# Four logit steps a unit instead of five, logits in five PSUM banks and half a borrowed one

## The chip, the cores and the metric

The kernel runs on one core of a Trainium2 chip. The core has a matrix engine (TensorE, PE in the profile; PEld are its weight loads), three engines for element-wise work (VectorE, DVE; ScalarE, ACT; GpSimd, POOL) and a queue that issues DMAs (SyncE, SP). They run at the same time and wait for each other by semaphores. Matmuls write to PSUM, eight banks of 512 fp32 columns on 128 partitions; DVE and ACT read PSUM, POOL and DMAs don't. The metric is the device time of one execution, in microseconds.

## What is computed

```python
xn = layernorm(x)                          # x: 2048 x 512, four segments of 512 rows
# A: attention with a memory; 32 heads of 16; for each segment
logits = q k^T / 4 + causal mask;  p = softmax(logits);  a_dot = p v
a_mem  = phi(q) M / (phi(q) z + 1e-6)      # phi(t) = t + 1 if t > 0 else exp(t)
o      = sigmoid(beta) a_mem + (1 - sigmoid(beta)) a_dot
M += phi(k)^T v;  z += sum of phi(k)       # carried to the next segment
s      = o wo
# B: g = silu(relu(xn w1) w2), w1: 512 x 1792
out = x + s * g
```

All in fp32. q, k, v are xn times wq, wk, wv (512 x 512).

## The kernel before

Matrix products in full precision are made of three fp32r matmuls of a number's high and low part (`triple`, lines 610 to 612): high x high, low x high, high x low. Weights come by DMA into `raw`, ACT copies the high part (L397), POOL subtracts for the low one (L398). The MLP (`mlp`), the projections of q and k (`proj`), values (`vproj`), output (`wout`) and memory (`memory`, `numden`) all run in this way on three PSUM banks `pd`.

The softmax works on *units* of four heads: 8 units a segment, 32 in all. A unit's rows stand in `qs` and `ks`, two heads in the two 64-row halves of the partitions and two planes p, put there by DMAs (`stack`, L909). Each row has a fourth part for its negative maximum, so that the exponential needs no other operand. So logits are made twice: first with queries as rows for the maxima (`rowmax`, into `pS`, two banks), then, with the maxima in place, transposed (`expo`, into `pT`, two banks), for ACT to take exponentials into `P` (L1026, L1020). Only blocks on and below the diagonal are made: widths 128, 256, 384 and 512. The two heads of a plane are a pair of matmuls that run side by side.

In `rowmax`, DVE reduces the part off the diagonal out of pS (L956), ACT copies the diagonal blocks to `rd` (L955), POOL masks these (L958), DVE reduces them (L961). At a unit's end DVE joins the maxima and splits them (L967 to L970), `maxrows` transposes them on PE (L977), ACT copies (L979), and two DMAs put them into qs. In `expo`, POOL clears what lies above the diagonal in P (L1016). `pv` multiplies P with the values into the bank `pO` (L1060); ACT scales (L1075), and DMAs and `combine` divide and merge with the memory's part.

A loop over steps t writes the order of PE: five steps a unit (tables RSTEP, ESTEP), in each the maxima's logits of unit u and the exponentials' logits of a unit LAG = 9 steps behind, and the values' product of a unit in two bursts (steps 0 and 2). Between these visits stands filler work, MLP and projections, dealt out by a budget. For the other engines a planner (class `Sched`) keeps a list of pending operations, each with a duration and a due time (the last number of `act`, `dve`, `pool`, `dma`), and writes the earliest due of those that could start. The semaphores are set later, from the order in which instructions touch tiles.

Of the kernel before, what the change touches and what calls it, by code (L numbers as in the profile page):

```python
# [7 lines left out]
F32 = mybir.dt.float32  # L8
# [17 lines left out]
LAG = 9  # L26
RESERVE = 13.00
M3 = 0.70
ND0 = 3
SOON = 0.21  # L30
SWITCH = 0.40


RSTEP = (((0, 3, 0),), ((0, 0, 0), (0, 2, 128)), ((0, 1, 0), (1, 1, 256)), ((1, 0, 0), (1, 2, 128)), ((1, 3, 0),))
ESTEP = (((0, 0, 0),), ((1, 0, 0),), ((0, 1, 0), (0, 3, 384)), ((1, 1, 0), (1, 3, 384)), ((0, 2, 0), (1, 2, 256)))
# [20 lines left out]
class Sched:  # L56
# [108 lines left out]
    def avail(self, rd, wr):  # L165
        t = 0.0
        ops = [self.W.get(k) for k in (*rd, *wr)]
        for k in wr:
            ops += self.R.get(k, ())
        for o in ops:  # L170
            if o is not None and o.eng != "PE":
                t = max(t, o.t if o.out else self.now + 3.31)
        return t
# [31 lines left out]
def emit(PE, ACT, DVE, POOL, SP, cst, ps, dr, args, plan, left):  # L205
# [38 lines left out]
    class Banks(Ring):  # L244

        def two(self):
            done = [(t, k) for t, k in self.t if k not in S.W or S.R.get(k)]
            return sorted(done, key=lambda b: S.avail((), (b[1],)))[:2]

        def next(self):  # L250
            return self.two()[0]

# [7 lines left out]
    S.free["POOL"] = 1.4  # L260
    identr = cst.tile([128, 128], F32R, name="identr")
    magic = cst.tile([128, 4], I32, name="magic")
    blk = cst.tile([128, 128], F32, name="blk")
    gcol = cst.tile([128, 4], F32, name="gcol")
# [10 lines left out]
    MM = [cst.tile([128, 128], F32R, name=f"mm{i}") for i in range(2)]  # L275
    Mbd = [cst.tile([128, 128], F32, name=f"mbd{g}") for g in range(4)]
    zbd = [cst.tile([128, 128], F32, name=f"zbd{g}") for g in range(4)]
# [5 lines left out]
    PDR = Banks("pd", [128, 512], F32, 3, ps)  # L283
    PSR = Ring("pS", [128, 2, 512], F32, 1, ps)
    PTR = Ring("pT", [128, 2, 512], F32, 1, ps)
    POR = Ring("pO", [128, 512], F32, 1, ps)
# [9 lines left out]
    EXR = Ring("ex", [128, L], F32)  # L296
# [4 lines left out]
    EER = Ring("ee", [128, L], F32)  # L301
# [9 lines left out]
    PR = [Ring(f"P{i}_", [128, 4, 512], F32) for i in range(2)]  # L311
# [6 lines left out]
    MV = Ring("mv", [128, 4, 2], F32, 2)  # L318
    RS = Ring("rs", [128, 4], F32, 2)
    NW = Ring("nw", [128, 2, 4], F32, 2)  # L320
# [5 lines left out]
    def consts():  # L326
        for i in range(NS):
            ks = stack_rows(i)
            pool(950, (), ks, lambda i=i: POOL.memset(r32(QS[i]), 0.0), 9.3 + 8 * i, 1e-3)
            pool(950, (), ks, lambda i=i: POOL.memset(r32(KS[i]), 1.0), 16.2 + 8 * i, 1e-3)  # L330
        pool(0, (), ["zrow"], lambda: POOL.memset(zrow, 0.0), 34.6)
        for i in range(2):
            pool(500, (), [f"mm{i}"], lambda i=i: POOL.memset(r32(MM[i]), 0.0), 51.4 + 5 * i, 1e-3)
        dve(128, (), ["identr"], lambda: DVE.tensor_copy(identr, ident), 53.4)
        for i in range(2):
            pool(500, (), [f"v{i}{t}" for t in range(4)],
                 lambda i=i: POOL.memset(VT[i][:, :, :, 16:32], 1.0), 33.1 + 20 * i, 1e-3)
        pool(100, (), ["blk"], lambda: POOL.memset(blk, 1.0), 46.8, 1e-3)
        b3 = blk.rearrange("p (b r) -> p b r", r=16)
        pool(128, ["blk"], ["blk"], lambda: POOL.affine_select(  # L340
            b3, b3, pattern=[[-16, 8], [0, 16]], compare_op=OP.is_ge, fill=0.0, base=0, channel_multiplier=1), 51.1)
        pool(128, ["blk"], ["blk"], lambda: POOL.affine_select(
            b3, b3, pattern=[[16, 8], [0, 16]], compare_op=OP.is_ge, fill=0.0, base=15, channel_multiplier=-1), 52.1)
        pool(10, (), ["magic"], lambda: POOL.memset(magic, 0x5f3759df), 66.0)

    def gates():
        for h in range(8):
            dma((), [f"gcol{h}"], lambda h=h: SP.dma_start(gcol[16 * h:16 * h + 16], bass.AP(
                tensor=beta.tensor, offset=beta.offset + h, ap=[[0, 16], [8, 4]])), 45.4)
        for b in range(4):  # L350
            dma((), [f"gsc{b}"], lambda b=b: SP.dma_start(gsc[32 * b:32 * b + 32], bass.AP(
                tensor=beta.tensor, offset=beta.offset + b, ap=[[0, 32], [4, 8]])), 47.5)
        pool(10, (), ["pari"], lambda: POOL.iota(pari, pattern=[[0, 2]], base=0, channel_multiplier=1), 53.8)
# [1022 lines left out]
```

## Time and profile before

| | us |
|---|---|
| median of 3 runs (lowest, highest) | 800.14 (797.95, 801.23) |
| profiled execution | 799.96 |
| its span, first to last instruction | 798.2 |
| PE busy | 767.3 |
| DVE, ACT, POOL busy | 474.7, 488.9, 484.8 |

Granted TensorE clock: 0.99 in the mean. A group row of the profile gives line, engine, operation, output<-inputs, shapes and count; then busy time and the mean length of one in ns; then idle time ahead of them with what ended it. A row of waits reads: who waited <- for whom: us in all, times, longest. fp32 matmuls stand in the trace as two records each.

### The profile page before, as it was taken

Reading aid. Unit: us, or ns where it says so; the run is one execution under the profiler, and the core shown is the slowest. Engines: PE = TensorE matmul, PEld = TensorE weight load, DVE = VectorE, ACT = ScalarE, POOL = GpSimd, SP = SyncE. Lnnn points to the kernel's source line nnn. Section 1 sums busy time; section 2 is a strip of 40 time slices with the busy share of each in tenths; the row PEclk is TensorE's granted clock in tenths of the full one; section 3 lists DMA queues with packets and bytes.
Section 4 is the critical chain, followed back from the end, with each engine's and each line's share of the span. In section 5 each row is a group of like instructions: output and inputs, shape, how many; then the busy total and the mean of one; then the engine's idle time right before and its main releaser. Section 6 shows DMA issues by size and latency. Waiting matters only on the chain.

```text
span 798.2 us, 14187 instructions
## 1 busy us (share of the span) xinstructions
PE 767.3 (96%) x4726; PEld 535.3 (67%) x4726; DVE 474.7 (59%) x838; ACT 488.9 (61%) x828; POOL 484.8 (61%) x585
## 2 busy tenths in 40 slices
PE   7999999999999999998999999999899989999996
PEld 6787677777676856575676766676576756665664
DVE  4336886546466765555655885664566445656546
ACT  4454757557766666567577576667367665665561
POOL 6735656556566555857467384866466566776474
PEclk9999999999999999999999999999899999999999
DMA  4345434355445445543454536544335447643233
GB/s 140 108 130 145 144 101 132 85 140 157 105 123 162 126 134 152 176 116 113 125 155 143 145 98 198 154 115 141 103 95 157 129 134 207 177 121 107 78 93 119
DMA packets 110632, 105.45 MB, mean 132 GB/s; under 512 B 23568, under 2 KB 73744, under 8 KB 110560
## 3 DMA queue, kind: packets, MB, share of 16 engines
q1 hardware_dynamic: 110480, 104.46, 45.2%
q8 instruction: 37, 0.61, 0.3%
q14 instruction: 35, 0.29, 0.1%
q10 hardware_dynamic: 80, 0.10, 0.0%
HBM read 65.44 MB, written 8.72 MB: 93 GB/s over the span
## 4 chain that ended last, share of the span: by engine, by line
PE 80%; DVE 5%; DMA 5%; POOL 4%; issue 4%; ACT 1%; SPq 1%; POOLq 0%; DVEq 0%; ACTq 0%
PE pd L610 19%; PE pd L611 15%; PE pd L612 15%; PE pO L1060 9%; PE pS L936 8%; PE pT L1009 4%; PE pd L595 4%; POOL wl L398 2%; PE pd L884 2%; DMA gsc<-in_A_beta_dram 1%; POOL rd L958 1%; DVE mn L956 1%; DVE hl L635 1%; PE pd L562 1%; PE pd L862 1%
## 5 line engine op out<-in xcount | busy, mean ns | idle before, releaser
L398 POOL TENSOR_TENSOR wl<-raw,wh 128x512 fp32r<-128x512 f32 x176 | 226.3, 1293 | 77.4 <-ACT wh L397 74.9
L956 DVE TENSOR_REDUCE mn<-pS 128x2 f32<-128x768 f32 (+2 forms) x160 | 127.0, 794 | 129.6 <-ACT rd L955 83.9
L958 POOL TENSOR_SCALAR_AFFINE_SELECT rd<-rd 128x512 f32<-128x512 f32 (+1 forms) x160 | 88.4, 553 | 153.1 <-ACT rd L955 151.0
L610 PE MATMUL pd<-xh,wh 128*128 128x512 f32 x352 | 147.6, 419 | 2.9 <-ACT vt L601 1.1
L955 ACT ACTIVATE rd<-pS 128x512 f32<-128x512 f32 (+1 forms) x160 | 82.0, 512 | 98.3 <-PE pS L936 85.6
L1026 ACT ACTIVATE P<-pT 128x1024 f32<-128x1024 f32 x128 | 131.1, 1024 | 15.0 <-PE pT L1009 14.0
L611 PE MATMUL pd<-xl,wh 128*128 128x512 f32 x352 | 137.7, 391 | 0.2 <-DVE xl L570 0.2
L612 PE MATMUL pd<-xh,wl 128*128 128x512 f32 x352 | 137.9, 392 | 0.0
L961 DVE TENSOR_REDUCE md<-rd 128x4 f32<-128x512 f32 (+1 forms) x160 | 92.0, 577 | 57.4 <-POOL rd L958 55.9
L397 ACT ACTIVATE wh<-raw 128x512 fp32r<-128x512 f32 x174 | 106.5, 630 | 10.1 <-DMA raw<-in_A_wk_dram 2.7
L1016 POOL TENSOR_SCALAR_AFFINE_SELECT P<-P 128x512 f32<-128x512 f32 x128 | 82.8, 656 | 35.1 <-ACT P L1026 31.0
L610 PE MATMUL pd<-wh,hh 128*128 128x512 f32 x224 | 95.4, 426 | 3.6 <-DVE kl L788 2.6
L936 PEld LDWEIGHTS pS<-ks,qs 64*128 64x128 f32 x512 | 40.7, 185 | 74.3 <-issue 40.2
L611 PE MATMUL pd<-wl,hh 128*128 128x512 f32 x224 | 88.0, 393 | 0.0
L612 PE MATMUL pd<-wh,hl 128*128 128x512 f32 x224 | 87.9, 393 | 0.0
L610 PEld LDWEIGHTS pd<-xh,wh 128*128 128x128 f32 x352 | 66.1, 188 | 30.8 <-issue 9.9
L936 PE MATMUL pS<-ks,qs 64*128 64x256 f32 (+3 forms) x512 | 83.9, 385 | 2.0 <-DVE mn L956 1.0
L1060 PE MATMUL pO<-P,vt 128*32 128x512 f32 (+3 forms) x1024 | 83.5, 442 | 0.8 <-POOL P L1016 0.8
L612 PEld LDWEIGHTS pd<-xh,wl 128*128 128x128 f32 x352 | 66.1, 188 | 14.8
L611 PEld LDWEIGHTS pd<-xl,wh 128*128 128x128 f32 x352 | 66.3, 188 | 11.3 <-DVE xl L570 0.5
L1009 PE MATMUL pT<-qs,ks 64*128 64x384 f32 (+3 forms) x512 | 64.7, 310 | 0.0
L610 PEld LDWEIGHTS pd<-wh,hh 128*128 128x128 f32 x224 | 42.1, 188 | 26.9 <-issue 7.6
(143 smaller groups left out, 1173.6 us busy)
## 6 DMA issues: line engine op xcount, KB each, us to landing
raw<-in_B_w_dram SPq DMA_DIRECT2D x112, 256.0 KB
qs<-qh SPq DMA_DIRECT2D x128, 64.0 KB
ks<-kh SPq DMA_DIRECT2D x128, 64.0 KB
io<-in_A_x_dram SPq DMA_DIRECT2D x28, 256.0 KB
raw<-in_A_wq_dram SPq DMA_DIRECT2D x16, 256.0 KB
raw<-in_A_wk_dram SPq DMA_DIRECT2D x16, 256.0 KB
raw<-in_A_wv_dram SPq DMA_DIRECT2D x16, 256.0 KB
qs<-ql SPq DMA_DIRECT2D x64, 64.0 KB
```

The costliest lines, as they stand in the source:

```text
L397: act(512, [rk], [hk], lambda: ACT.activation(h, raw, AF.Copy), 6.3)
L398: pool(512, [rk, hk], [lk], lambda: POOL.tensor_tensor(l, raw, r32(h), op=OP.subtract), 32.9)
L610: PE.matmul(pt, st_, mv_, start=first, stop=False)
L611: PE.matmul(pt, st_, ml, start=False, stop=False)
L612: PE.matmul(pt, sl, mv_, start=False, stop=last)
L936: PE.matmul(pS[:, a, o:o + w], qs[r, p, w - 128:w], ks[r, p, :w], start=True, stop=True)
L956: dve(512 if n == 2 else 768, [pk], [f"{nk}.{k}"], lambda: DVE.tensor_reduce(on, nd, axis=AX.X, op=OP.max, negate=True), 3.9, banks=("S",))
L958: pool(256 * n, [rk], [rk], lambda: POOL.affine_select(R, R, pattern=[[0, 2 * n], [-1, 128]], compare_op=OP.is_ge, fill=-3.0e38, base=0, c ...
L961: dve(256 * n, [rk], [f"{dk}.{k}"], lambda: DVE.tensor_reduce(od, R4, axis=AX.X, op=OP.max, negate=True), 1.1)
L1009: PE.matmul(pT[:, a, o:o + w], ks[r, p, 128 * i:128 * i + 128], qs[r, p, 128 * i:], start=True, stop=True)
L1026: act(1024, [tk], [both[p]], lambda: ACT.activation(P[:, 2 * p:2 * p + 2, :], pT, AF.Exp, scale=0.25), 0.5)
L1060: PE.matmul(pO[32 * b:32 * b + 32, 128 * i:], v, P[:, b, o:o + w], start=i == 0, stop=i == 2)
```

## The change

- **Banks.** All eight banks are one tile `ps` (PSB; PL is the same by columns). Logits use banks 0 to 4 and one of 5 to 7, borrowed for the step; the other banks serve as `pd`. pO is gone: `pv` writes into one of 5 to 7.
- **Steps.** Four a unit, two for each plane p, with four pairs in each: two of maxima (R) and two of exponentials (E) of different units, LAG = 8. Of one pair in each step (R 1 or E 2) one head goes to bank 0 and the other to the borrowed bank; DVE or ACT reads both with one instruction (`both`).
- **Maxima.** DVE adds a mask (`cmask`) to the diagonal blocks straight from PSUM into rd (L991) and reduces rd (L1007); off the diagonal it reduces from PSUM (L994, L999, L1002). ACT's copy and POOL's masking of rd are gone.
- **Exponentials.** Four ACT instructions a plane (768, 512, 1024, 256 columns: L1043, L1046, L1050, L1052) into one P, laid out in blocks of 128.
- **Values.** One burst of 16 matmuls a unit behind step 0 of the next.
- **q and k.** ACT copies the projection to SBUF (L807), POOL rounds (L808) and subtracts (L821); the phi functions read the copy.
- zbd is made when needed; `proj` is called for q and k apart; the row DMAs of `stack` are sent by plane; due times and budgets have other numbers.

```diff
-RSTEP = (((0, 3, 0),), ((0, 0, 0), (0, 2, 128)), ((0, 1, 0), (1, 1, 256)), ((1, 0, 0), (1, 2, 128)), ((1, 3, 0),))
-ESTEP = (((0, 0, 0),), ((1, 0, 0),), ((0, 1, 0), (0, 3, 384)), ((1, 1, 0), (1, 3, 384)), ((0, 2, 0), (1, 2, 256)))
+STEP = (
+    (("R", 3, 12, 16), ("E", 1, 4, 8), ("E", 2, 0, None), ("R", 0, 7, 11)),
+    (("E", 0, 8, 16), ("R", 2, 4, 12), ("R", 1, 0, None), ("E", 3, 7, 15)),
+)
+PAT = (slice(6, 10), slice(1, 4), slice(0, 5, 4), slice(5, 6))
...
-    PDR = Banks("pd", [128, 512], F32, 3, ps)
-    PSR = Ring("pS", [128, 2, 512], F32, 1, ps)
-    PTR = Ring("pT", [128, 2, 512], F32, 1, ps)
-    POR = Ring("pO", [128, 512], F32, 1, ps)
+    PSB = ps.tile([128, 8, 512], F32, name="ps")
+    PL = PSB.rearrange("q b w -> q (b w)")
+    PDR = Banks("pd", [(PSB[:, b, :], f"pd{b}") for b in (5, 6, 7)])
...
-            act(512, [pk], [thk], lambda th=th, pp=pp: ACT.activation(th, pp, AF.Copy), 6.1)
-            dve(512, [pk, thk], [tlk], lambda th=th, tl=tl, pp=pp: DVE.tensor_tensor(
-                tl, pp, r32(th), op=OP.subtract), 31.0)
+            tf = r32(tl)
+            act(512, [pk], [tlk], lambda tf=tf, pp=pp: ACT.activation(tf, pp, AF.Copy), 0.0)
+            pool(512, [tlk], [thk], lambda th=th, tf=tf: POOL.tensor_copy(th, tf), 1.8, 1e-3)
...
+            pool(512, [thk, tlk], [tlk], lambda th=th, tl=tl, tf=tf: POOL.tensor_tensor(
+                tl, tf, r32(th), op=OP.subtract), 8.4)
...
+    def logits(u, v, k, bank, then):
+        p, x = divmod(k, 2)
+        at1 = 4 * int(bank[2:]) if bank else None
...
+        S.pe(0.30 * len(wr), rd, wr + ([bank] if bank else []), go)
+        if then:
+            then()
+        bk = [bank] if bank else []
+        if u is not None:
+            rowmax(u, k, bk, at1)
+        if v is not None:
+            expo(v, k, bk, at1)
+
+    def both(at1, n, o=0):
+        return PSB[:, 0:8 if at1 is None else at1 // 4 + 1:1 if at1 is None else at1 // 4, 128 * o:128 * (o + n)]
...
+            return lambda: DVE.tensor_tensor(out, ps, cmask[:, None, :].to_broadcast([128, n, 128]), op=OP.add)
+
+        if x == 0:
+            dve(768, [pk], [f"{nk}.{k}"], lambda: DVE.tensor_reduce(
+                mn[:, p, :, 3], PSB[:, 3:5, :384], axis=AX.X, op=OP.max, negate=True), 3.7, banks=(3, 4))
+            dve(512, [pk, "cmask"], rks, masked(4, R, PLU[:, 7:20:4, :]), 0.0, banks=(1, 2, 3, 4))
         else:
+            dve(512, [pk], [f"{nk}.{k}"], lambda: DVE.tensor_reduce(
+                mn[:, p, :, 2], PSB[:, 1:5:2, :256], axis=AX.X, op=OP.max, negate=True), 0.7, banks=(1, 3))
+            dve(256, [pk, "cmask"], rks[1:], masked(2, R[:, 2:4], PLU[:, 6:20:8, :]), 2.6, banks=(1, 3))
+            dve(256, [pk, *bk], [f"{nk}.{k}2"], lambda: DVE.tensor_reduce(
+                mn[:, p, :, 1], both(at1, 1), axis=AX.X, op=OP.max, negate=True), 1.1, banks=(0,))
+            dve(256, [pk, "cmask", *bk], rks[:1], masked(2, R[:, 0:2], both(at1, 1, 1)), 2.2, banks=(0,))
...
+            act(512, [tk, *bk], [f"{pk}a"], lambda: ACT.activation(
+                put(2), both(at1, 2).rearrange("q a (u w) -> q a u w", w=128), AF.Exp, scale=0.25), 0.3, banks=(0,))
...
+                    PE.matmul(pO[32 * b:32 * b + 32, 128 * i:].rearrange("q (u w) -> q u w", w=128), v,
+                              P[:, b // 2, PAT[i], b % 2, :], start=i == 0, stop=i == 3)
```

How the order of instructions moves, at three places. [waits X] names the engines (or DMA queues) whose counts an instruction waits for.

PE before, in the middle of the program: the first burst of values of a unit with a visit to the logits behind it, then the next filler work (`vproj`).

```order
L1060 MATMUL pO_123<-P_0_171,vt_88 32x512 [waits Pool_49]
L1060 MATMUL pO_123<-P_0_171,vt_88 32x512 x3
L936 MATMUL pS_121<-ks_85,qs_81 128x128 x2
L936 MATMUL pS_121<-ks_85,qs_81 128x384 x2
L1009 MATMUL pT_122<-qs_79,ks_83 128x384 x2
L1009 MATMUL pT_122<-qs_79,ks_83 128x128 x2
L595 MATMUL pd_120<-wh_111,xh_129 128x256 [waits Activation_49]
```

PE after the change, a step 0: four pairs, then the whole product of the values.

```order
L957 MATMUL ps<-ks_87,qs_83 128x512
L960 MATMUL ps<-qs_81,ks_85 128x384 [waits DMAHW7_49]
L960 MATMUL ps<-qs_81,ks_85 128x384
L960 MATMUL ps<-qs_81,ks_85 128x256
L960 MATMUL ps<-qs_81,ks_85 128x256 [waits Activation_49]
L957 MATMUL ps<-ks_87,qs_83 128x128 x2
L1076 MATMUL ps<-P,vt_89 32x512 [waits Activation_49,Pool_49]
L1076 MATMUL ps<-P,vt_89 32x512
L1076 MATMUL ps<-P,vt_89 32x512 [waits Pool_49]
```

What moved: a visit has four pairs where the ones before have two to four, a unit has four visits where it had five, and the values follow one of them in one burst.

PE after the change, the odd step next to it: the last pairs of the visit, and the filler group that follows (a projection into one bank, 12 matmuls that add up).

```order
L957 MATMUL ps<-ks_87,qs_83 128x256
L957 MATMUL ps<-ks_87,qs_83 128x256 [waits Activation_49]
L960 MATMUL ps<-qs_81,ks_85 128x128 x2
L627 MATMUL ps<-xh_121,wh_109 128x512 [waits Activation_49]
L628 MATMUL ps<-xl_123,wh_109 128x512
L629 MATMUL ps<-xh_121,wl_114 128x512
L627 MATMUL ps<-xh_121,wh_109 128x512
L628 MATMUL ps<-xl_123,wh_109 128x512
L629 MATMUL ps<-xh_121,wl_114 128x512
L627 MATMUL ps<-xh_121,wh_109 128x512 [waits DVE_49]
```

What moved: the seventh matmul of the group has a wait for DVE, though its bank and its operands are those of the six before it.

DVE after the change, the readers of that same visit and the end of the step before.

```order
L991 TENSOR_TENSOR rd_150<-ps,cmask 128x512 [waits PE_49]
L1138 TENSOR_TENSOR nn_164<-nn_164,dd_165 128x512 [waits DMAHW0_49,Pool_49]
L994 TENSOR_REDUCE mn_155<-ps 128x2 [waits Activation_49]
L1007 TENSOR_REDUCE md_153<-rd_150 128x2x2 [waits DVE_49]
L999 TENSOR_REDUCE mn_155<-ps 128x2 [waits PE_49,Activation_49]
L1002 TENSOR_REDUCE mn_155<-ps 128x2 [waits PE_49,Activation_49]
L991 TENSOR_TENSOR rd_151<-ps,cmask 128x256 [waits Activation_49]
L991 TENSOR_TENSOR rd_151<-ps,cmask 128x256
L819 SCALAR_TENSOR_TENSOR pq_135<-ql_132,pq_135 128x512 [waits Activation_49]
L1007 TENSOR_REDUCE md_153<-rd_151 128x2x2 [waits DVE_49]
```

What moved: the work on rd, which ACT and POOL did, stands in DVE's queue, and the reads of the pair (L1002, the first L991 behind it) wait for PE and ACT besides. By their counts, L1002 waits for the sixth matmul of the filler group above, ACT's L1052 for L1002, L991 for L1052, and the seventh matmul for L991.

670 lines of the change are left out of this document (328 added, 342 removed).

## The prediction

> **What bounds the kernel now.** I read the page first, for busy shares.
>
> ```profile
> span 798.2 us, 14187 instructions
> PE 767.3 (96%) x4726; PEld 535.3 (67%) x4726; DVE 474.7 (59%) x838; ACT 488.9 (61%) x828; POOL 484.8 (61%) x585
> PE 80%; DVE 5%; DMA 5%; POOL 4%; issue 4%; ACT 1%; SPq 1%; POOLq 0%; DVEq 0%; ACTq 0%
> ```
>
> PE is busy for 767.3 of 798.2 us, and the chain that ended last is PE for 80%; every other engine is near 60%. So I asked what PE waits for (the waits on PE: us in total, times, longest).
>
> ```profile
> PE pd L977 <- DVE hl L635: 4.5, 2, 3.1
> PE pS L936 <- DVE mn L956: 1.0, 2, 0.6
> PE pS L936 <- ACT rd L955: 0.9, 1, 0.9
> DVE mn L956 <- ACT rd L955: 83.9, 54, 6.9
> ```
>
> The largest wait on PE is 4.5 us. The first logit matmul of a step hardly ever waits for its readers (1.0 and 0.9 us). The last row I keep for later: DVE waits 83.9 us for ACT's copy L955, though both only read pS, so two engines that read one bank are made to take turns. As PE is full, the next view is PE's timeline, for what its time consists of (start, us, instruction, records in a row).
>
> ```profile
> 485.60 1.50 PE L1060 MATMUL pO<-P,vt 128*32 128x384 f32 x24
> 487.03 0.49 PE L936 MATMUL pS<-ks,qs 64*128 64x512 f32 x2
> ...
> 488.96 0.39 PE L612 MATMUL pd<-wh,ol 128*128 128x512 f32 x1
> ...
> 489.66 0.40 PE L612 MATMUL pd<-wh,ol 128*128 128x512 f32 x1
> 489.99 0.50 PE L936 MATMUL pS<-ks,qs 64*128 64x512 f32 x2
> 490.32 0.40 PE L1009 MATMUL pT<-qs,ks 64*128 64x512 f32 x2
> 490.65 0.50 PE L610 MATMUL pd<-wh,oh 128*128 128x512 f32 x1
> 490.99 0.39 PE L611 MATMUL pd<-wl,oh 128*128 128x512 f32 x1
> ...
> 494.13 1.07 PE L1060 MATMUL pO<-P,vt 128*32 128x512 f32 x8
> 495.12 0.55 PE L936 MATMUL pS<-ks,qs 64*128 64x128 f32 x4
> ```
>
> From 488.96 to 489.66 three 512-column matmuls start: 0.233 us each. From 489.66 to 490.99 there are two of them and two pairs of logits, 4 x 0.233 = 0.93 us of streaming (a pair runs side by side), and 1.33 us pass. So **a visit to the logits costs 0.40 us** over its streaming.
>
> **The change, part by part.**
>
> *Fewer visits.* PE issues the same matmuls but for the warm-up. A unit has four visits of four pairs where it had five; with the lead (LAG) and the last values there are 128+8+1 = 137 where there were 160+9+1 = 170. 33 x 0.40 = -13.2 us.
>
> *Values in one burst.* 512 columns take 0.99 us (494.13 to 495.12) and 768 take 1.43 (485.60 to 487.03): 0.11 us a burst and 0.00172 us a column. 32 bursts fewer: -3.5 us. That their moving operand is now in pieces of 128 columns costs nothing in the nearest row: L884 reads pieces of 16 columns.
>
> ```profile
> 104.16 0.89 PE pd L884 x8
> L459 PE MATMUL pO<-ident 128*128 128x128 f32 x38 | 8.4, 401 | 1.4 <-POOL epst L259 1.4
> ```
>
> Its eight records (two to a matmul of 128 columns) take 0.89 us where 4 x 128 x 0.00172 makes 0.88: at most 0.0025 us for each of 320 pieces, under 1 us; I take 0. The warm-up loses 6 matmuls, 12 of 38 records of 8.4 us: 2.7 us at most, nothing if the first DMAs end later; -1.
>
> Together PE is 17.7 us lighter.
>
> *Maxima on DVE, q and k on POOL.* I price the new instructions by their lengths.
>
> ```profile
> L956 DVE TENSOR_REDUCE mn<-pS 128x2 f32<-128x768 f32 x64 | 61.1, 955 | 46.7 <-PE pS L936 31.0 <-ACT rd L955 15.5
> L956 DVE TENSOR_REDUCE mn<-pS 128x2 f32<-128x512 f32 x64 | 44.0, 688 | 67.3 <-ACT rd L955 56.8 <-PE pS L936 10.2
> L961 DVE TENSOR_REDUCE md<-rd 128x2 f32<-128x256 f32 x64 | 26.5, 416 | 24.3 <-POOL rd L958 23.7
> L955 ACT ACTIVATE rd<-pS 128x512 f32<-128x512 f32 x96 | 57.5, 599 | 72.7 <-PE pS L936 62.7 <-issue 1.7 <-POOL wl L398 1.6
> L955 ACT ACTIVATE rd<-pS 128x256 f32<-128x256 f32 x64 | 24.5, 382 | 25.6 <-PE pS L936 22.9 <-DVE mn L956 2.4
> L1026 ACT ACTIVATE P<-pT 128x1024 f32<-128x1024 f32 x128 | 131.1, 1024 | 15.0 <-PE pT L1009 14.0
> L612 PE MATMUL pd<-xh,wl 128*128 128x512 f32 x352 | 137.9, 392 | 0.0
> ```
>
> An even step gives DVE 0.96 (768) + 0.69 (masking 512) + 0.69 (maxima of 512), an odd one 0.69 + 3 x 0.42 + 0.69: 4.97 us a half, 64 halves, 318 us, where L956 and L961 take 219. Without L788 (22 us) DVE comes to about 552 us, 69%. ACT loses the copies L955 (82.0 us) and gains 16 by its exponentials (0.81, between the rows, + 0.60 + 1.02 + 0.38 = 2.81 a half, where it had two and a half of 1.02). POOL trades 88 us of masking for 61 of splitting. None is full, so **as load this costs nothing**, and PE's work is the cover; if DVE lost that cover it would be the bound, which is the second rival.
>
> The split of q and k now runs ACT, POOL, POOL before the row DMAs, about 1.2 us longer than with DVE, and stack is issued two steps ahead of its logits. Twelve DMAs leave SP for it, ordered so that the half needed first leaves first. The bounds are 0 and one late half a projection; I take 0, since filler work stands between.
>
> *The borrowed bank.* This decides. Banks 0 to 7 are now one tile, ps. In an odd step DVE reads the pair of bank 0 and the borrowed bank b by one instruction (both()), in an even step ACT does. The waits in the program are set by the range that a pattern spans, not by the two banks: reading 0 and 7 counts as touching 1 to 6. The rows of the order shown with the change tell it: an L627 in the middle of its accumulation waits for DVE, whose L1002 waits for PE. Following each wait's count to the instruction that reaches it, I find 59 places where PE's matmul n releases such a read, and PE's matmul n+1 waits until the read is done; in 54 of them it writes a bank that the read does not touch. Nothing can hide such **a hairpin**: nothing of PE's work stands between. PE started every 0.233 us; now it must let matmul n finish (0.39 us, L612's row), hand over, wait for the read, and be released. The nearest row for a hand-over is at the start of the run, where PE really waits so.
>
> ```profile
> 13.73 0.45 PE pd L562 x4
> 14.18 0.02 issue
> 14.21 0.61 ACT xh L569
> 14.81 0.02 issue
> 14.84 0.70 DVE xl L570
> 15.54 0.04 issue
> 15.58 0.50 PE pd L611
> ```
>
> A hand-over takes 0.03 us. So a hairpin costs the read + 0.39 - 0.23 + 0.06 = the read + 0.22 us:
>
> - 27 over one ACT exponential of 512 (0.60): 0.82 each, 22.1 us
> - 19 over one DVE read of 256 (0.42): 0.64 each, 12.2 us
> - 9 over DVE, ACT's 1024, DVE (0.42 + 1.02 + 0.42 + 0.06): 2.14 each, 19.3 us
> - 4 over DVE, ACT's 256, DVE (0.42 + 0.38 + 0.42 + 0.06): 1.50 each, 6.0 us
>
> Together 59.6 us; by the reads and their hand-overs alone 46, the lower bound; with 14 more places where an older matmul releases the read, at 0.4 us, 65. PE's idle time of now, 798.2 - 767.3 = 31 us, may fall into these holes in part: I take 10 off. The same turns lengthen an odd step's readers to a row, DVE 0.69 and 0.42, ACT 0.38, DVE 0.42 and 0.42, ACT 1.02: 3.4 us and five hand-overs, 3.5. 40 odd steps leave fewer than 16 filler matmuls (16 x 0.233 = 3.7 us) until the next visit; if none of them held a hairpin they would lack about 28 us together, if all did, nothing: +8.
>
> [...]
>
> **The sum.** 798.2 - 17.7 + 59.6 - 10 + 8 = 838.1 us of span. The runs' median lies 800.14 - 798.2 = 1.9 above this span: **840 us**, 5% slower.
>
> **The rivals.**
>
> *The hairpins cost nothing that counts: 782 us.* Then PE's saving is all: 798.2 - 17.7 + 1.9. For it speaks that PE now waits for logit banks 1.9 us in all; against it, that a hairpin leaves no matmul to run meanwhile. It decides for faster if a hairpin costs under 17.7 / 59 = 0.30 us, less than the shortest read. Chance 0.12.
>
> *DVE becomes the bound: about 848 us.* Per unit DVE has 4.97 x 2 for maxima, 1.3 for L967 to L970 (16.0 + 11.7 + 13.5 us over 32), and (552 - 318 - 41) / 32 = 6.0 other work, 17.2 us. It also waits: in two odd steps for a PE triple (0.7) and ACT (0.4), in two even steps for ACT's 0.60, one of which follows the values' 2.4: 5.8 us. 23.0 us x 34 units (32 and the lead) = 782; the time before the first logits (45.6) and after the last values (798.2 - 779.7 = 18.5), 64; with 1.9, 848. For it: all DVE work runs in one queue, so what waits holds the rest. Against: waits of DVE may fall where it has nothing to do anyway. Chance 0.22.
>
> ```profile
> 45.60 0.50 PE L936 MATMUL pS<-ks,qs 64*128 64x512 f32 x2
> ...
> 778.15 1.50 PE L1060 MATMUL pO<-P,vt 128*32 128x384 f32 x24
> ...
> L967 DVE TENSOR_TENSOR md<-md,mn 128x12 f32<-128x12 f32 x32 | 16.0, 500 | 0.4
> L969 DVE CAST mm<-md 128x16 fp32r<-128x16 f32 x32 | 11.7, 366 | 0.5
> L970 DVE TENSOR_TENSOR mm<-md,mm 128x16 fp32r<-128x16 f32 x32 | 13.5, 422 | 0.5
> ```
>
> *Gain and hairpins cancel: about 797 us.* The reads alone (46), all of PE's 31 us of idle time falling into them, no late visit: 798.2 - 17.7 + 46 - 31 + 1.9. Chance 0.07: much of the idle time lies at the start and the end, where no hairpin is.
>
> That the change does not do what it says I leave out: the order rows show four visits and one burst.
>
> **How the numbers follow.** The forecast has 0.59, with its own range 815 to 874: reads alone (46), 10 off and 0 late visits give 818; 65, all 28 of late visits and nothing off give 876. The range 800 to 874 holds nearly all of the forecast, most of the DVE rival (above it where DVE's waits exceed those listed) and some of the third. One measurement of this kernel tells 0.5% from no change, 4 us: faster 0.12 (the first rival), same 0.07 (the third), slower 0.81.
>
> **What would show it.** In the changed profile, PE's waits should name L991 and L1002 (DVE) and L1046 (ACT) ahead of L627, about 50 us in all, and these should be matmuls in the middle of a group. PE's busy time should fall below 755 us although the span grows. A logit visit should cost 0.40 us still. If DVE is the bound, its busy share stays near 70% but logit matmuls L957 and L960 wait for it by tens of us. The forecast is wrong if waits ahead of L627 sum to under 20 us.

## The result, and the profile after

The changed kernel takes 895.69 us (median of 5 runs, 887.71 to 899.31) beside 801.23 us (797.95 to 802.38) for the one before: ratio 1.1163, interval 1.1127 to 1.12. It is 12% slower, where 5% was forecast, and outside the range. The page of the profiled execution (887.71 us) begins:

```profile
span 886.0 us, 14268 instructions
PE 779.8 (88%) x4714; PEld 556.1 (63%) x4714; DVE 542.2 (61%) x998; ACT 435.3 (49%) x764; POOL 465.5 (53%) x490
```

PE now idles for 106 us where it idled for 31. DVE, ACT and POOL have the loads that the prediction worked out (552, 423, and 458 from its 484.8 - 88 + 61) within 3%. What PE waits for, in the columns of the prediction (us in all, times, longest):

```profile
PE ps L627 <- DVE rd L991: 32.1, 26, 2.1
PE ps L627 <- ACT P L1046: 15.6, 22, 0.9
PE ps L612 <- DVE rd L991: 8.7, 6, 2.1
PE ps L627 <- DVE mn L1002: 5.5, 9, 0.9
PE ps L957 <- issue: 5.2, 9, 1.2
PE ps L1022 <- DVE mm L1016: 3.9, 2, 2.2
PE ps L579 <- ACT io L511: 3.6, 1, 3.6
```

The first, second and fourth row sum to 53.2 us. These are mostly the hairpins, at the lines where the prediction put them. One of the nine long ones, on the timeline of the changed kernel (start, us, instruction; the last bracket is idle time and its releaser):

```profile
359.19 0.40 PE L629 MATMUL ps<-wh,hl 128*128 128x512 f32 x1
359.52 0.50 PE L960 MATMUL ps<-qs,ks 64*128 64x512 f32 x2
359.85 0.46 PE L957 MATMUL ps<-ks,qs 64*128 64x384 f32 x4
360.14 0.23 PE L960 MATMUL ps<-qs,ks 64*128 64x128 f32 x2
360.29 0.50 PE L627 MATMUL ps<-xh,wh 128*128 128x512 f32 x1
360.63 0.39 PE L628 MATMUL ps<-xl,wh 128*128 128x512 f32 x1
360.85 0.39 PE L629 MATMUL ps<-xh,wl 128*128 128x512 f32 x1
361.35 0.42 DVE L1002 TENSOR_REDUCE mn<-ps 128x2 f32<-128x256 f32 x1 [1.03 <-PE ps L629]
361.81 1.02 ACT L1050 ACTIVATE P<-ps 128x1024 f32<-128x1024 f32 x1 [1.02 <-DVE mn L1002]
362.86 0.42 DVE L991 TENSOR_TENSOR rd<-ps,cmask 128x256 f32<-128x256 f32 x1 [1.09 <-ACT P L1050]
363.34 0.50 PE L627 MATMUL ps<-xh,wh 128*128 128x512 f32 x1 [2.10 <-DVE rd L991]
363.68 0.40 PE L628 MATMUL ps<-xl,wh 128*128 128x512 f32 x1
...
365.11 0.63 PE L627 MATMUL ps<-xh,wh 128*128 128x512 f32 x1
365.53 0.63 PE L628 MATMUL ps<-xl,wh 128*128 128x512 f32 x1
```

L629 at 360.85 lets DVE's read go, DVE lets ACT, ACT lets DVE, and the next filler matmul, on a bank that none of them touches, starts at 363.34: 2.49 us start to start for 0.23. Then something that the prediction hadn't: from 365.11 on, matmuls start 0.42 us apart and last 0.63. The view of stretches of 3.4 us shows why (PE busy with its number of records, then PEld, DVE, ACT, POOL; the column with 1.00 or 0.50 is the granted clock):

```profile
357.70:361.10 3.40, 3.40 (x20) 2.34 (x18) 1.57 (x4) 0.83 (x2) 1.08 (x3) 1.00 0.74 230
361.10:364.50 3.40, 1.30 (x6) 0.98 (x6) 2.03 (x5) 1.02 (x1) 0.64 (x1) 1.00 0.10 20
364.50:367.90 3.40, 3.40 (x11) 2.18 (x9) 1.28 (x5) 1.27 (x3) 0.61 (x2) 0.50 0.06 10
```

The stretch with the hairpin has PE busy for 1.30 of 3.40 us, and in the next the clock is 0.50. In the middle of the run the clock is at half in seven such stretches, 23.9 us, so 12 us lost; before it was 10.2 us, 5 lost. Five of the seven follow a hairpin over DVE, ACT's 1024, DVE like this one; one follows PE's wait of 2.2 us for L1016 (the sixth row of waits above), one a wait of 1.56 us for L991. The five runs of the changed kernel, by their length:

| span, us | mean granted clock | span x (1 - clock), us |
|---|---|---|
| 886.0 | 0.977 | 20 |
| 891.6 | 0.973 | 24 |
| 894.0 | 0.976 | 21 |
| 895.5 | 0.968 | 29 |
| 897.6 | 0.964 | 32 |

From the shortest to the longest run the span grows by 11.6 us and the lost clock time by 12. But the clock isn't all: the run of 894.0 us, the median, lost 1 us more to the clock than the shortest and is 8 us longer. (The last column also holds half clock at the start and the end, 16 us of it in the profiled run.) The profiled run is the shortest; why the median lies 8 us above it stays open.

### The profile page after: what moved, and what is told of

It reads as the page before. It is cut to its first block, busy times and chain, and to the rows that moved or that the text cites. A ratio compares the mean times of both kernels' runs of the same rounds, so it can differ in the third digit from the quotient of the medians.

```text
span 886.0 us, 14268 instructions
## 1 busy us (share of the span) xinstructions
PE 779.8 (88%) x4714; PEld 556.1 (63%) x4714; DVE 542.2 (61%) x998; ACT 435.3 (49%) x764; POOL 465.5 (53%) x490
## 5 line engine op out<-in xcount | busy, mean ns | idle before, releaser
L627 PE MATMUL ps<-xh,wh 128*128 128x512 f32 x352 | 151.1, 429 | 24.2 <-DVE rd L991 12.4
L991 DVE TENSOR_TENSOR rd<-ps,cmask 128x256 f32<-128x256 f32 (+1 forms) x192 | 95.0, 508 | 82.9 <-ACT P L1046 33.4
L629 PE MATMUL ps<-xh,wl 128*128 128x512 f32 x352 | 140.0, 398 | 0.0
L628 PE MATMUL ps<-xl,wh 128*128 128x512 f32 x352 | 139.7, 397 | 0.0
L627 PE MATMUL ps<-wh,hh 128*128 128x512 f32 x224 | 98.5, 440 | 28.0 <-DVE rd L991 16.5
L1046 ACT ACTIVATE P<-ps 128x512 f32<-128x512 f32 x64 | 38.3, 598 | 158.6 <-PE ps L629 64.0
L627 PEld LDWEIGHTS ps<-xh,wh 128*128 128x128 f32 x352 | 67.1, 190 | 55.3 <-DVE rd L991 17.6
L629 PE MATMUL ps<-wh,hl 128*128 128x512 f32 x224 | 88.8, 397 | 0.0
L628 PE MATMUL ps<-wl,hh 128*128 128x512 f32 x224 | 88.5, 395 | 0.0
L1007 DVE TENSOR_REDUCE md<-rd 128x4 f32<-128x512 f32 x128 | 86.6, 679 | 1.0
L994 DVE TENSOR_REDUCE mn<-ps 128x2 f32<-128x768 f32 x64 | 61.0, 954 | 42.5 <-ACT P L1046 42.5
L957 PE MATMUL ps<-ks,qs 64*128 64x512 f32 (+3 forms) x512 | 78.5, 340 | 9.4 <-issue 5.2
L1050 ACT ACTIVATE P<-ps 128x1024 f32<-128x1024 f32 x64 | 65.7, 1026 | 39.5 <-DVE mn L1002 28.6
L960 PE MATMUL ps<-qs,ks 64*128 64x384 f32 (+3 forms) x512 | 78.4, 338 | 3.7 <-DVE mn L994 1.5
L627 PEld LDWEIGHTS ps<-wh,hh 128*128 128x128 f32 x224 | 42.1, 188 | 55.5 <-DVE rd L991 21.6
L629 PEld LDWEIGHTS ps<-xh,wl 128*128 128x128 f32 x352 | 67.2, 191 | 15.3
L628 PEld LDWEIGHTS ps<-xl,wh 128*128 128x128 f32 x352 | 67.5, 192 | 10.0
L957 PEld LDWEIGHTS ps<-ks,qs 64*128 64x128 f32 x512 | 49.8, 188 | 37.2 <-issue 18.7
```

Of the source, the lines that this page charges most:

```text
L627: PE.matmul(pt, st_, mv_, start=first, stop=False)
L628: PE.matmul(pt, st_, ml, start=False, stop=False)
L629: PE.matmul(pt, sl, mv_, start=False, stop=last)
L957: PE.matmul(PL[:, 128 * at[a]:128 * at[a] + w], QS[u % NS][r, p, b], KS[u % NS][r, p, :w], start=True, stop=True)
L960: PE.matmul(PL[:, 128 * at[a]:128 * at[a] + w], KS[v % NS][r, p, b], QS[v % NS][r, p, 128 * i:], start=True, stop=True)
L991: return lambda: DVE.tensor_tensor(out, ps, cmask[:, None, :].to_broadcast([128, n, 128]), op=OP.add)
```

## The experiments

Theory A: the range that a read spans makes the hairpins, and these make all that follows. Theory B: DVE's load, or the row in which the readers stand, sets the pace. All edits change what an instruction in a given place does or touches; unless said otherwise the order on every engine, and TensorE's program, stay as in the changed kernel. The kernel before took 799.1 to 799.9 us beside these runs.

### The reads split, all or in part

Each read of the pair becomes two instructions of one bank each (`e_split`, below the split kernel), or only DVE's two reads (`e_dve`), or only ACT's (`e_act`).

```diff
+    half = lambda at1, a, n, o=0: PSB[:, a * at1 // 4:a * at1 // 4 + 1, 128 * o:128 * (o + n)]
...
-            dve(256, [pk, *bk], [f"{nk}.{k}2"], lambda: DVE.tensor_reduce(
-                mn[:, p, :, 1], both(at1, 1), axis=AX.X, op=OP.max, negate=True), 1.1, banks=(0,))
+            dve(256, [pk, *bk], [f"{nk}.{k}2"], lambda: [DVE.tensor_reduce(
+                mn[:, p, a:a + 1, 1], half(at1, a, 1), axis=AX.X, op=OP.max, negate=True) for a in (0, 1)], 1.1, banks=(0,))
-            dve(256, [pk, "cmask", *bk], rks[:1], masked(2, R[:, 0:2], both(at1, 1, 1)), 2.2, banks=(0,))
+            dve(256, [pk, "cmask", *bk], rks[:1], lambda: [masked(1, R[:, a:a + 1], half(at1, a, 1, 1))() for a in (0, 1)], 2.2, banks=(0,))
...
-            act(512, [tk, *bk], [f"{pk}a"], lambda: ACT.activation(
-                put(2), both(at1, 2).rearrange("q a (u w) -> q a u w", w=128), AF.Exp, scale=0.25), 0.3, banks=(0,))
+            act(512, [tk, *bk], [f"{pk}a"], lambda: [ACT.activation(
+                put(2)[:, a:a + 1], half(at1, a, 2).rearrange("q a (u w) -> q a u w", w=128), AF.Exp, scale=0.25) for a in (0, 1)], 0.3, banks=(0,))
```

> Each read of bank 0 and the borrowed bank (L1002, the second L991, L1046) becomes two instructions, one for each bank; every engine keeps its order, and TensorE's program is the same. Of the 62 places where a matmul waits for a read that the matmul before released, 3 are left. Theory A (the range that a read spans makes the holes, and the holes make what follows them): in the changed kernel's trace the 59 holes cost about 65 us over streaming, the matmul after each starts some 0.1 us late (6 us), and the clock is at half for about 20 us more than before (10 us); so 895.7 - 81 = 815 us at most, and down to 780 if the visits that come late are late because of them. The new instructions cost ACT 0.17 us and DVE 0.16 us for each read split (11 and 20 us), which lies beside TensorE. Rival B (the readers stand in a row and this row sets the pace, DVE above all): the row grows by 0.3 to 0.5 us in each step, so 880 us or more, and TensorE's waits move from L627 to L957 and L960.

> Only DVE's two reads of the pair (L1002, the second L991) are split; ACT's L1046 still spans the banks between. 30 of the 62 places are left, 27 of them over ACT. Theory A: the 32 holes over DVE (41.8 us over streaming in the trace of the changed kernel) go, with 3 us of late restarts and half of the clock's 10: 895.7 - 50 = 846 us, between 835 and 855. Rival B: DVE has 20 us more to do, so 885 to 915.

> Only ACT's read of the pair (L1046) is split; DVE's L1002 and L991 still span the banks between. 35 of the 62 places are left, 32 of them over DVE. Theory A: the 27 holes over ACT (22.8 us over streaming) go, with 3 us of late restarts and near half of the clock's 10: 895.7 - 30 = 866 us, between 855 and 875; the savings of this run and of the one that splits DVE's reads add up to that of both within 10 us. Rival B: ACT's even step grows by 0.17 us, DVE's row is as it was: within 10 us of 895.7.

Measured: all split 786.51 us (785.57 to 788.82; ratio to before 0.9841, 0.9802 to 0.9881); only DVE's split 818.09 (1.0234, 1.0196 to 1.0271); only ACT's split 856.92 (1.0727, 1.0675 to 1.0778). PE in the split kernel:

```profile
PE 750.0 (95%) x4714; PEld 551.3 (70%) x4714; DVE 543.5 (69%) x1126; ACT 433.9 (55%) x828; POOL 463.2 (59%) x490
```

So 109 us hang on these three instructions, and the kernel without hairpins is 1.6% faster than the one before, with 128 more instructions on DVE and 64 more on ACT. Theory B, by which it should have taken 880 us or more, is out. The parts save 77.6 and 38.8 us, 116 together for 109. Where DVE's reads alone are left whole (`e_act`, the first rows), the waits on PE are those of the changed kernel without the ACT row; where ACT's alone is (`e_dve`, the row after them), nearly all that is left of them is ACT's row:

```profile
PE ps L627 <- DVE rd L991: 32.3, 26, 2.1
PE ps L612 <- DVE rd L991: 8.7, 6, 2.1
PE ps L627 <- DVE mn L1002: 5.5, 9, 0.9
```

```profile
PE ps L627 <- ACT P L1046: 17.7, 23, 1.5
```

Theory A held, but its sizes for the parts were short: 77.6 for 50 (DVE's) and 38.8 for 30 (ACT's).

TensorE's program is the same in the changed kernel and in the split one, so the two traces can be laid side by side from visit to visit: 135 stretches, in which the changed kernel loses 101 us (up to the first visit it is 2 us ahead).

| what stands in the stretch | stretches | forecast for it, us | gap on PE over 0.23, mean | lost in the stretch, median |
|---|---|---|---|---|
| one hairpin over ACT's 512 | 23 | 0.82 | 0.88 | 0.98 |
| one over DVE's L1002 | 2 | 0.64 | 0.78 | 0.81 |
| one over DVE's L991 | 3 | 0.64 | 0.87 | 1.13 |
| DVE, ACT's 256, DVE | 4 | 1.50 | 1.75 | 1.71 |
| DVE, ACT's 1024, DVE, clock stays | 4 | 2.14 | 2.23 | 2.39 |
| the same, half clock behind it | 5 | 2.14 | 2.23 | 3.69 |
| none | 83 | | | 0.04 |

The gaps are means over all hairpins of the kind (26, 9, 9, 4, 9); two more stretches with one over ACT's 512 have half clock in them, one of them also the wait for L1016, and lose 2.60 in the median; the other nine are mixed, most of them with two hairpins. A stretch with one hairpin loses its gap and about 0.1 us more: the matmul behind it takes 0.34 us to the next start (363.34 to 363.68 above) where others take 0.23. The stretches with none mostly lose nothing, but 28 of them lose 0.4 us or more, 26 us in all. There PE often waits for L991 at the end of a row of readers: the first logit matmul of a visit (L957), or a filler matmul whose read an older matmul had released. The profile names no releaser for such an L957, but it starts 0.1 us after L991 has ended (799.72):

```profile
799.31 0.41 DVE L991 TENSOR_TENSOR rd<-ps,cmask 128x256 f32<-128x256 f32 x1
799.83 0.50 PE L957 MATMUL ps<-ks,qs 64*128 64x512 f32 x2 [1.17 <-issue]
```

Matmul by matmul (start to start in the changed kernel less the same in the split one) the 98.9 us of span between the two profiled runs (886.0 and 787.1; the medians lie 109 apart) are:

| where | us |
|---|---|
| 57 matmuls held by a hairpin | 61.4 |
| the matmul after each of these | 5.2 |
| matmuls at half clock, one of them held by a hairpin too | 10.6 |
| first logit matmuls of a visit that start within 0.2 us of the end of L991 (11 are late) | 7.3 |
| 7 other filler matmuls that wait for L991, released by an older matmul as far as the trace tells | 9.6 |
| other filler matmuls that wait, 2.3 of it for L1016 | 8.5 |
| the rest (the time up to the first visit among it) | -3.7 |

### DVE's load taken away

The largest reduction of DVE is cut to a third, in the changed kernel (`e_light`) and in the split one (`e_slight`).

```diff
             dve(768, [pk], [f"{nk}.{k}"], lambda: DVE.tensor_reduce(
-                mn[:, p, :, 3], PSB[:, 3:5, :384], axis=AX.X, op=OP.max, negate=True), 3.7, banks=(3, 4))
+                mn[:, p, :, 3], PSB[:, 3:5, :128], axis=AX.X, op=OP.max, negate=True), 3.7, banks=(3, 4))
```

> The largest reduction of DVE (L994) reads 128 of its 384 columns in each bank (a third of these maxima is left out, so the output is not the reference's): 0.42 for 0.95 us, 64 times, 34 us less work for DVE; all else as in the changed kernel, the reads across the banks too. Theory A: the holes don't care, less than 8 us (888 to 897), since DVE's load is beside TensorE. Rival B: if DVE's row of readers is the pace, most of the 34 us comes back: 860 to 870.

> As the split kernel, but the largest reduction of DVE (L994) reads 128 of its 384 columns in each bank (a third of these maxima is left out, so the output is not the reference's): 34 us less work for DVE. If DVE's load costs at the rate of 14 us for 35, as the added work showed: 773 us; if it costs only once it is above what the split kernel has: 784 to 787.

Measured: 888.54 us (884.92 to 889.86), 7 less than the changed kernel; and 787.68 (784.85 to 789.17), as the split one. Some 33 us less of DVE's work (510.4 for 542.2 us in `e_light`, 508.9 for 543.5 in `e_slight`) buy nothing where there are no hairpins, and some 7 us where there are, though the runs of the two kernels overlap there. DVE isn't the bound.

### One of DVE's two reads left whole

In the split kernel the masking read is whole again (`e_mn`), or the reduction is (`e_rd`): the second or the first pair of the diff of the split reads undone.

> As the split kernel, but DVE's masking read of the pair (the second L991) is one instruction again. 27 more of the places than in the split kernel, each over this one read of 256 columns; the chains through ACT are gone, since the first read of the pair (L1002) doesn't span. Theory A (each hole costs the read and its hand-over, and only a hole near 2 us long drops the clock): 27 x (0.87 + 0.10) = 26 over 786.5, 812 us, between 807 and 818, and no stretch of half clock in the middle that the split kernel hasn't. Rival C (DVE's two reads each make half of the 70 us by which the kernel with both whole lies above the split one): 821.

> As the split kernel, but DVE's reduction of the pair (L1002) is one instruction again, the masking read split. 26 more places than in the split kernel, each over one read of 256 columns. Theory A: 26 x (0.78 + 0.10) = 23 over 786.5, 809 us, between 804 and 816; so the two single reads together give 49 us where both at once gave 70, and the rest comes from the 13 chains over DVE, ACT, DVE and the clock that they drop. Rival C: 821.

Measured: 812.44 us (810.90 to 813.44) for `e_mn`, as theory A has it; 819.71 (818.54 to 821.40) for `e_rd`, 4 above its band. The hairpins of the second are no longer than reckoned (16.3 us of waits in 26):

```profile
PE ps L627 <- DVE mn L1002: 13.2, 21, 0.9
PE ps L612 <- DVE mn L1002: 3.1, 5, 0.7
PE ps L957 <- DVE rd L991: 1.7, 2, 1.1
```

But L1002, first of the pair's readers, now waits for filler matmuls (L629) and for ACT, whose banks lie in its range. The rows of all waits in `e_rd`:

```profile
DVE mn L1002 <- PE ps L629: 26.1, 20, 3.2
...
DVE mn L1002 <- ACT P L1052: 22.0, 15, 4.2
...
DVE mn L1002 <- ACT P L1050: 10.8, 10, 1.2
```

In the split kernel L1002 has one row of waits, and it is for the logit matmuls of its own visit (L960 is the visit's last pair):

```profile
DVE mn L1002 <- PE ps L960: 22.1, 21, 3.8
```

Laid beside the split kernel as above, the stretches of `e_rd` that hold no hairpin lose 11 us: the row of readers ends later, and the first logit matmuls of 11 visits start 6 us later in all. That is the part that theory A had left out of its price.

With both reads whole (`e_act`) the loss was 70 us against the split kernel, with either alone 26 and 33. The 11 us between go with the chains (the hairpins over DVE, ACT, DVE), which need both: in `e_act` the clock dropped to half seven times in the middle, six times right behind a chain over ACT's 1024 and once within one; in `e_mn` and `e_rd`, with hairpins of at most 1.1 us, it never did.

### The same instructions on other banks

In `r574` no instruction is added, resized or moved against the changed kernel. The four whole logit banks are 0 to 3, the half-used one is 6, the borrowed ones are 5, 7 and 4.

```diff
-    (("R", 3, 12, 16), ("E", 1, 4, 8), ("E", 2, 0, None), ("R", 0, 7, 11)),
...
+    (("R", 3, 8, 12), ("E", 1, 0, 4), ("E", 2, 24, None), ("R", 0, 3, 7)),
...
-    PDR = Banks("pd", [(PSB[:, b, :], f"pd{b}") for b in (5, 6, 7)])
+    PDR = Banks("pd", [(PSB[:, b, :], f"pd{b}") for b in (5, 7, 4)])
...
-        return PSB[:, 0:8 if at1 is None else at1 // 4 + 1:1 if at1 is None else at1 // 4, 128 * o:128 * (o + n)]
+        return PSB[:, min(6, at1 // 4):max(6, at1 // 4) + 1:abs(6 - at1 // 4), 128 * o:128 * (o + n)]
```

> The changed kernel with its instructions, their sizes and the order on every engine as they are; only the numbers of the PSUM banks differ. The four whole logit banks are 0 to 3, the half-used one is 6, and the borrowed ones are 5, 7 and 4 (for 5, 6 and 7), so that a read of the pair spans just the two banks except where 4 is borrowed, when it spans 5 too. 13 of the 62 places are left (the split kernel has 3), none of them a chain. Theory A: ten holes of about 0.97 us more than the split kernel, but none of its added reads (20 us of DVE, which at the 14 us that 35 us of added DVE work cost may be worth 8): 788 us, between 782 and 797. If the time came from the load, from the number of reads or from the four steps as such, and not from the span, the kernel stays near 895 us.

Measured: 797.68 us (795.28 to 800.25), ratio to before 0.9978 (0.9957 to 0.9999). Bank numbers alone are worth 98 us. The place shown above, on its timeline:

```profile
336.86 0.51 PE L627 MATMUL ps<-xh,wh 128*128 128x512 f32 x1
336.94 0.43 DVE L1002 TENSOR_REDUCE mn<-ps 128x2 f32<-128x256 f32 x1
...
337.26 1.02 ACT L1050 ACTIVATE P<-ps 128x1024 f32<-128x1024 f32 x1
337.28 0.41 DVE L991 TENSOR_TENSOR rd<-ps,cmask 128x256 f32<-128x256 f32 x1
...
338.81 0.39 PE L629 MATMUL ps<-xh,wl 128*128 128x512 f32 x1
...
339.04 0.39 PE L627 MATMUL ps<-xh,wh 128*128 128x512 f32 x1
```

DVE starts L1002 (336.94) 0.08 us behind the first filler matmul (336.86) instead of 1.06 (360.29 to 361.35), L991 no longer waits for ACT's L1050 but runs beside it, and the filler matmul of the hairpin (339.04) follows its predecessor by 0.23 us.

Then the reads that still span a bank between (where 4 is borrowed) are split as well, as above (`r574s`), and on top of that the first three weights get back their due time of the kernel before (`r574x`, this edit alone):

```diff
-            7.8 if early else 4.0, 3.5)
+            22.2 if early else 4.0, 3.5)
```

> As the kernel with other bank numbers, and where bank 4 is borrowed (its read would span bank 5) the read is two instructions. 3 of the 62 places are left, as in the split kernel, with few added reads. Theory A: ten holes less than with the bank numbers alone, 778 to 787 us. If the added reads of the split kernel cost nothing: 786.5.

> As the last, and the first three weights have their due time of the kernel before (22.2 for 7.8), so that the planner issues x first and puts POOL's normalisation of the second tile ahead of its work on the weights. Theory A: TensorE starts its first real matmul near 6 us for 10.7 and isn't held up at the second tile; 2 to 5 us less than the last. Rival: some other wait takes it up: within 1.5 us of the last.

Measured: 787.07 us (784.14 to 792.00) for `r574s` and 780.64 (780.11 to 780.95) for `r574x`. The last ten hairpins cost 10.6 us, 1.06 each, with a few us of scatter in `r574s`. `r574s` is level with the split kernel (786.51), though it has few of its added reads: these cost nothing that shows. `r574x` is the best: ratio to before 0.9759 (0.9729 to 0.9788).

### The start

`e_start` is the split kernel with SP's first seven DMAs in another order, x ahead of the weights, and no other engine's order touched.

```diff
-        dma((), [rk], lambda: SP.dma_start(raw.rearrange("p (k f) -> p k f", k=kn) if kn else raw, src),
-            7.8 if early else 4.0, 3.5)
+        issue = lambda: SP.dma_start(raw.rearrange("p (k f) -> p k f", k=kn) if kn else raw, src)
+        dma((), [rk], (lambda: late.append(issue)) if early else issue, 7.8 if early else 4.0, 3.5)
...
-            dma((), [k], lambda xt=xt, t=t: SP.dma_start(xt, x2[s * L + 128 * t:s * L + 128 * (t + 1), :]),
-                8.8 if s == 0 else 8.0, (1.8, 2.7, 2.8, 3.0)[t] if s == 0 else 4.5)
+            dma((), [k], lambda xt=xt, t=t: [SP.dma_start(xt, x2[s * L + 128 * t:s * L + 128 * (t + 1), :])] + [
+                late.pop(0)() for _ in range(len(late) if t == 3 else 0)], 8.8 if s == 0 else 8.0, (1.8, 2.7, 2.8, 3.0)[t] if s == 0 else 4.5)
```

> As the kernel with all three reads split (786.5 us), but SP issues the four DMAs of x first and the three weights behind them; the other engines' instructions and orders are the same. In the trace of the split kernel the first x tile is there at 8.1 us, in the kernel before at 3.3 us, and TensorE's first real matmul starts at 10.67 where it started at 5.86: 4.8 us. Theory A: this is why the split kernel lies 4 us above the 782 us that the lighter TensorE alone would give; with x first, 782 to 783.5 (the weights land 2 us later, which may take a little back). Rival: the first weights or POOL's splitting of them decide the start, or later waits take up the gain: 785 to 787.

Measured: 786.19 us (780.88 to 788.25), the rival; of its four runs one, 780.88, lies below what either expected. The split kernel's start, and then what PE waits for in `e_start`:

```profile
2.38 1.93 SPq L486 DMA_DIRECT2D io<-in_A_x_dram  x4
...
8.09 0.69 DVE L492 BATCH_NORM_STATS2 st<-io 128x6 f32<-128x512 f32 x1 [8.09 <-DMA io<-in_A_x_dram]
...
10.67 1.11 PE L579 MATMUL ps<-ident,io 128*128 128x128 f32 x4 [4.63 <-ACT io L511]
```

```profile
PE ps L579 <- POOL io L508: 5.6, 1, 5.6
```

POOL has the weights' rounding and subtraction in its queue ahead of the normalisation of the second x tile (L508), and the weights now come later: the same wait, one tile on. In `r574x` the planner knows that x comes first and puts L508 ahead:

```profile
0.79 1.81 SPq L486 DMA_DIRECT2D io<-in_A_x_dram  x4
...
5.93 0.66 PE L579 MATMUL ps<-ident,io 128*128 128x128 f32 x4 [0.16 <-ACT io L511]
...
7.19 0.76 POOL L508 TENSOR_SCALAR io<-io,rs,nb 128x512 f32<-128x512 f32 x1 [5.79 <-DVE nb L505]
```

That is 4.7 us earlier than in the split kernel for the first real matmul, and 5.2 earlier than in `r574s` (11.09); beside `r574s` the time is 6.4 us less. The planner's later order differs in this kernel too, so not all of the 6.4 need be the start's.

### The split of q and k on DVE

In the split kernel L808 and L821 go to DVE instead of POOL, in the same place of the program (`e_qk`).

```diff
-            pool(512, [tlk], [thk], lambda th=th, tf=tf: POOL.tensor_copy(th, tf), 1.8, 1e-3)
+            pool(512, [tlk], [thk], lambda th=th, tf=tf: DVE.tensor_copy(th, tf), 1.8, 1e-3)
...
-            pool(512, [thk, tlk], [tlk], lambda th=th, tl=tl, tf=tf: POOL.tensor_tensor(
+            pool(512, [thk, tlk], [tlk], lambda th=th, tl=tl, tf=tf: DVE.tensor_tensor(
```

> As the split kernel, but the rounding and subtraction of q and k go to DVE in place of POOL (64 instructions of 512 columns, 30 to 45 us more work for DVE, 543 to about 580 of 787 us). Theory A: DVE's load lies beside TensorE; 786.5 within 3 us. Rival B (DVE is next to being the bound): most of the added work shows, 805 to 825.

Measured: 800.66 us (797.88 to 804.24), 14 more, between the two. DVE goes from 543 to 580 us, and the waits are for what DVE delivers late:

```profile
PE ps L1022 <- DVE mm L1016: 5.3, 3, 4.2
PE ps L957 <- issue: 5.1, 5, 1.9
...
PE ps L957 <- DMA ks<-kl: 3.5, 2, 2.6
```

So 36 us more on DVE cost 14 where 34 less bought nothing. The moved instructions also stand in DVE's queue between others: in one place L821, 1.22 us long, comes ahead of L1015 and L1016, for which L1022 waits. This run doesn't tell the load from the place in the queue.

## Why the prediction was wrong in size

The direction, the mechanism and the place were right; the sum fell short by 56 us of median, 48 of them in the profiled span (886.0 for 838.1). The steps that failed are those around the hairpins: the idle time taken off (-10), and four terms put at nothing or nearly so: the matmuls at half clock, the filler matmuls that wait through an older matmul's release, the slow restart behind each hairpin and the late first DMAs. The hairpins' own price was nearly right.

**Visits and burst: held.** Above, from L629 at 359.19 to L628 at 360.63 1.44 us pass; two filler matmuls and pairs of 512 + 384 + 256 + 128 columns stream for 2304 x 0.233 / 512 = 1.05. A visit costs 0.39 us still, for 0.40. A burst of the values takes 2.30 us where the two took 2.42:

```profile
368.62 2.36 PE L1076 MATMUL ps<-P,vt 128*32 128x512 f32 x32
370.92 0.50 PE L627 MATMUL ps<-xh,wh 128*128 128x512 f32 x1
```

The kernel with neither hairpins nor the late start is 18.8 us below the one before (799.44 - 780.64); the prediction's lighter PE was 17.7. The first rival's time, 782, is about what the change would have given without both.

**Warm-up: the step failed.** It allowed for first DMAs that end later, but priced none. The edited due times put three weights ahead of x on SP, and the first real matmul starts at 9.68 us in the changed kernel's profiled run, 10.67 in the split kernel's, for 5.86 before: 5 to 6 us off the term of -1. The split kernel's profiled span, 787.1, is 6.6 above the prediction's 798.2 - 17.7.

**Extra load: held**, by the two runs with less of it; by `e_qk` perhaps with little to spare. That the split of q and k costs nothing wasn't measured by itself.

**The price of a hairpin: up to 5 us short.** 65 us of gaps for 59.6, 61 of them beside the split kernel, where a few of these matmuls wait too. ACT's 512 came out within 0.06 us (0.88 for 0.82); those over one DVE read took 0.14 and 0.23 us more than forecast, the chains 0.09 and 0.25. The slow restart, the 0.1 us that the matmul behind each hairpin takes longer to the next start, wasn't in the sum: 5 us.

**Idle time that falls into the holes, -10: wrong.** Hardly anything was absorbed. Stretches with a hairpin lose all of it (0.98 for 0.88), since no matmul is free to run meanwhile, which the prediction itself said of a hairpin. The split kernel, with the same order, idles for 37 us in other places.

**Late visits, +8: about right for what it named**, 7.3 us at the first logit matmuls. What was left out is beside it: filler matmuls that wait for L991 through an older matmul's release lost 9.6 us at 7 places; the prediction knew of 14 such places, at 0.4 us, and had them in its upper bound alone. Other filler matmuls that wait lost 8.5. That all these are late because of the wide reads is shown for them together, since they go when the reads are split; no run takes one of these groups away alone.

**The clock: not in the sum.** Matmuls at half clock lose 10.6 us beside the split kernel; beside the kernel before, 7 us more are lost to half clock in the middle (12 for 5). The 8 us by which the median run lies above the profiled one aren't explained by it: that run's clock is 0.976 for 0.977.

**The sum again**, for the profiled span: 1.8 (hairpins, 61.4 for 59.6) + 10 (idle time) + 5.2 (restart) + 10.6 (half clock) - 0.7 (late visits) + 9.6 (older releases) + 8.5 (other waits) - 3.7 (the rest) + 6.6 (the split kernel above the forecast, its late start above all) make the 47.9 us.

The range's ends, 815 and 874, aren't the 818 and 876 that the prediction works out beside them, and the second of those sums to 875; 895.69 lies above all of them.

**The rivals.** DVE as the bound (848) was wrong: some 33 us less of its work changed little. Cancelling (797) was wrong with the absorbed idle time. Of what was to be seen, L627's waits summed to 53 us for about 50; PE's busy time was to fall under 755 us, and read 779.8, since a matmul ahead of a hole is busy for 0.39 us where the next used to start after 0.23, and those behind holes (0.50 at 363.34) and at half clock (0.63 at 365.11) last longer; without the hairpins it is 750.0.

**Whether the waits are needed** isn't shown. The split kernel, whose reads of the pair span one bank each, gives 786.5 us; the waits themselves weren't taken away from a read that spans the banks, so what that would do on the chip is open.

## What to carry to other kernels

In this kernel an access to several banks by one strided instruction was held against all the banks between (the filler matmul at 363.34, on a bank that no such read touches, stood 2.10 us for L991): put the banks that are read together next to each other, or read them apart. Here the added short reads cost nothing that shows (786.51 us with all of them, 787.07 with few), and each wide read alone cost 26 to 33 us, the three together 109. Count the places where a matmul waits for a read that the matmul just before it released: no other idle time filled these here, each cost its read, the hand-overs and a slow restart (0.98 us in the median for one over ACT's 512), and at 12 of the 18 chains of 2.10 us the clock dropped to half as well, directly behind a hairpin under 1.2 us in the changed kernel never. When due times are edited, look at the first ten DMAs: what stood ahead of the first operand put off the first real matmul by 5.2 us in `r574s` beside `r574x`, and the time by up to 6.4.

## What the hardware showed that I had not expected

The granted clock changed on a grid: in each trace all its changes in the middle of the run lie a whole number of 3.41 us apart. In the changed kernel the six stretches on the grid, between 360 and 760 us, in which PE was busy for 36 to 42% were all followed by half clock; five of them held one hole of 2.10 us, at least 1.96 of it. The emptiest that was not (the first row, the second is the stretch behind it) had 51%, and its hole was of the same kind, cut by the grid's edge:

```profile
494.20:497.60 3.40, 1.72 (x8) 1.43 (x9) 2.18 (x6) 1.02 (x1) 1.22 (x2) 1.00 0.29 68
497.60:501.00 3.40, 3.40 (x30) 1.96 (x32) 2.28 (x6) 0.00 (x0) 0.00 (x0) 1.00 0.00 0
```

Of the 18 chains over ACT's 1024 in the changed kernel and in `e_act`, each a hole of 2.10 us, 11 had at least 1.9 us of it within one stretch of the grid, and all 11 were followed by half clock. Of the seven that the grid's edge cut further, one was; its stretch (498.1 to 501.5 in `e_act`) had PE busy for 56%. Of the hairpins under 1.2 us in the changed kernel, none was followed by it directly. So a gap of 2.10 us was enough here, and what told was how much of one stretch was idle rather than the gap alone, though no one share divides them: PE was busy for 54% of the stretch at 804.8 us, with a hole of 1.56, and half clock followed; for 52% of the one at 425.9, with a hole of 1.65, and none followed. Whether the times differ from run to run because the grid falls otherwise on the same holes wasn't shown: 8 us lie between two runs of the changed kernel with clocks of 0.977 and 0.976, and in the split kernel the longest of four runs (787.1 us) has the highest clock, 0.997.
